# Decayed attention and a gated FFN on one core: loads, masks, weights and fillings moved at once

## The chip, the cores and the metric

The kernel runs on one core of a Trainium2 chip. The metric is the device time of one execution in microseconds (us); lower is better. The core has five engines that each run their own list of instructions strictly in order: TensorE (PE, with its weight loads as PEld), VectorE (DVE), ScalarE (ACT), GpSimd (POOL) and SyncE (SP). They meet only at semaphores. DMAs are issued from POOL (a software queue) or from SP (a hardware queue) and carried out by 16 DMA engines.

## The reference

Eight batches of eight heads, 576 positions, 64 wide; then a feed-forward block over all 4608 tokens of width 512. Cut to what matters:

```python
# attention: q, k, v (8, 8, 576, 64), f (8, 8, 576)
scores = q @ k.T / sqrt(64)
cum = cumsum(log(clip(f, 1e-4, 1)))
scores = where(causal, scores + cum[i] - cum[j], -1e9)
x = softmax(scores) @ v                    # tokens x (8*64 = 512)
# ffn: w_gate, w_val (512, 1536), w_out (1536, 512), rms_g (512)
xn = x / sqrt(mean(x*x) + 1e-6) * rms_g
g = xn @ w_gate
out = (g * sigmoid(g) * (xn @ w_val)) @ w_out      # (4608, 512) float32
```

## The kernel before

**Attention.** The decay exp(-cum[j]) does not depend on the query row, and exp(cum[i]) cancels in the softmax. So the kernel never adds the decay to the scores. At the start it works out `dec` = exp(-cum) for all 64 pairs of batch and head (f is loaded at L233; logarithm L257, scan L263, exp L268, transposed on PE at L277), and multiplies v by it (`scale_v`, L421; L422 writes the decay itself as a 65th column, which gives the denominator). A batch has five rows of 128 queries, j = 0 to 3 and a last one of 64. For each row and half of the heads come the scores on PE (L446), exp on ACT (L464), the mask of the diagonal block on POOL (L471, an affine select that writes zeros), the products with the scaled values on PE (L490), and a division by the 65th column on DVE (L504, L506), which gives a tile x of 128 tokens by 512.

q and k must stand transposed for the scores. For batches 0 and 1 PE does it (L392, L398, copied at L405); for the others SP issues DMA transposes (L377).

**Norm and FFN.** ACT squares x and adds up a row (L522); POOL divides by 512, adds 1e-6 (L526) and raises to the power -0.5 (L527); ACT scales x with it to xn (L534). xn is then transposed to xT: on PE with a copy by DVE for token groups 0 and 1 (L542, L550, L552), with DMA transposes from SP for the rest (L556). A token group g below 8 is the first 512 tokens of batch g; group 8 gathers the last 64 tokens of each batch (tile xTr). For every group PE multiplies xT with w_gate and w_val (L601), ACT takes a tanh (L613), DVE makes ga (L615) and hT (L608) of it, PE projects hT with w_out (L626), ACT copies the result out of the bank (L631), and SP stores it (L634). The products of both gates and of the projection, the transposes and the values share four accumulation banks ("ff"); the scores have two of their own.

**The RMS weights.** rms_g multiplies along the width of x. In group 0 the copy of xT does it (L550). After group 0 the function `weigh` (L340) multiplies both weight matrices in place, 24 operations of 128 x 512 on DVE, each third as soon as group 0 has used it; later groups then copy plainly.

**Loads and queues.** `load_qk` (L298) loads 128 rows of q or k, `load_qk2` (L310) 256 rows of them, `load_v` (L321) 128 rows of v, `load_w` (L331) a third of w_gate and of w_val, `load_wo` (L346) half of w_out. All are issued by POOL but the v of batch 1 and the first tile of batch 0, which SP issues. On each queue a DMA waits until the one eight before it has landed. Tiles for v are four in turn, those for scaled values two.

**The order.** The kernel builds a list of units, each with an engine, an assumed duration, a key and the tiles it takes and gives back. `Plan` plays them through on paper, at each step giving a free engine the unit with the lowest key that is ready, with a small random share in every key from a fixed seed. The units are then written out in that order, which each engine keeps. `fill` (L676) writes products of a constant tile ahead of units that by the plan leave PE idle in the first 25 us.

Of the kernel before, what the change touches and what calls it, by code (L numbers as in the profile page):

```python
# [10 lines left out]
F32 = mybir.dt.float32  # L11
# [6 lines left out]
class Unit:  # L18


    def __init__(self, eng, dur, key, emit, lat):
        self.eng, self.dur, self.key, self.emit, self.lat = eng, dur, key, emit, lat
        self.need, self.then, self.take, self.give = 0, [], [], []
# [9 lines left out]
class Plan:  # L33
# [20 lines left out]
    def fits(self, u):  # L54
        want = [h for h in u.take if h.slot is None]
        for h in want:
# [4 lines left out]
            elif n < sum(w.ring == h.ring for w in want):  # L61
                return False
# [12 lines left out]
    def run(self):  # L75
# [8 lines left out]
        draw = random.Random(149)  # L84
# [58 lines left out]
def fox_ffn_kernel(ctx, tc, q, k, v, f, moe_w_gate, moe_w_val, moe_w_out, moe_rms_g, out):  # L143
# [4 lines left out]
    NB = 5  # L148
# [10 lines left out]
    def ring(name, n, shape, dt, pool=sb):  # L159
# [3 lines left out]
                 sc=2, ff=4, hw=8, sw=8)  # L163
# [8 lines left out]
    T_x = ring("x", sizes["x"], [128, DM], F32)  # L172
# [18 lines left out]
    junk = sb.tile([128, DM], BF16, name="junk")  # L191
    warm = sb.tile([128, 128], BF16, name="warm")
    one = sb.tile([BH, 1], F32, name="one")
    mid = sb.tile([BH, 1], F32, name="mid")
    tmp = T_hT[1].rearrange("p f t -> p (f t)").bitcast(F32)
    fr, cum, dec = (tmp[0:BH, i * 640:i * 640 + n] for i, n in enumerate((S, S, NB * 128)))
    stat = [sb.tile([128, B, NB], F32, name=n) for n in ("sq", "ms", "rs")]
# [29 lines left out]
    PLAIN = 1  # L227

# [18 lines left out]
    def emit_ident():  # L247
        make_identity(nc, ident_f)
        nc.gpsimd.memset(mhalf, -0.5)

    dve(0.18, -30, lambda: nc.vector.memset(warm, 1.0))
    iden_f = pool(0.7, -15.5, emit_ident)
    iden = dve(0.23, -19, lambda: nc.vector.tensor_copy(ident, ident_f), [iden_f])

    d1 = dve(0.5, -19, lambda: nc.vector.tensor_scalar(fr, in0=fr, scalar1=1e-4, op0=ALU.max, scalar2=1.0,
                                                       op1=ALU.min), [L_f])
    d2 = act(0.7, -19, lambda: nc.scalar.activation(fr, fr, ACT.Ln), [d1])  # L257

    def emit_cum():
        ones = bass.AP(tensor=one.tensor, offset=one.offset, ap=[one.ap[0], [0, S]])  # L260
        nc.vector.memset(one, 1.0)
        nc.vector.memset(dec[:, S:], 0.0)
# [4 lines left out]
    d3 = dve(2.5, -19, emit_cum, [d2])  # L267
    d4 = act(0.9, -19, lambda: nc.scalar.activation(dec[:, 0:S], cum, ACT.Exp, scale=-1.0, bias=mid[:, 0:1]),  # L268
# [11 lines left out]
    d5 = pe(0.6, -19, emit_dect, [d4, iden_f], take=[h_dec])  # L280
    L_dec = dve(0.45, -19, lambda: nc.vector.tensor_copy(
# [32 lines left out]
    def load_v(b, j, key):  # L314
# [3 lines left out]
        eng, queue, dur = ("POOL", nc.gpsimd, 0.9) if b != 1 and b + j else ("SP", nc.sync, 0.6)  # L318
# [8 lines left out]
    def load_w(i, key):  # L327
        c0, c1 = i * 512, (i + 1) * 512
        for w, src, nm in ((wg, moe_w_gate, "g"), (wv, moe_w_val, "v")):
            def emit(w=w, src=src):  # L330
                nc.gpsimd.dma_start(out=w[:, :, c0:c1], in_=src[:, c0:c1].rearrange("(c p) f -> p c f", p=128))  # L331
            Lw[nm, i] = [load("POOL", 0.75, (512, 0.0061), key, emit, late=2.6)]

    def weigh(i, key, deps):

        c0, c1 = i * 512, (i + 1) * 512
        for w, nm in ((wg, "g"), (wv, "v")):
            def emit(w=w):
                for dc in range(NDC):
                    nc.vector.tensor_scalar_mul(w[:, dc, c0:c1], w[:, dc, c0:c1], rgT[:, dc:dc + 1])  # L340
            Lw[nm, i] = [dve(1.3, key, emit, deps[nm])]

    def load_wo(key):
        for i in range(2):
# [4 lines left out]
            Lo.append(load("POOL", 0.85, (768, 0.0061), key, emit))  # L349


    for at, (j, two) in ((-16, (0, False)), (-15, (1, True)), (-13, (3, False))):
        (load_qk2 if two else load_qk)(0, j, at)
        for i in range(j, j + 1 + two):
            load_v(0, i, at + 0.01)
    load_w(0, -14)
    load_w(1, -12)
    load_w(2, -11)
    load_wo(-9.25)
    for j in (0, 2):  # L360
        load_qk2(1, j, -9.5 + j * 0.1)
        load_v(1, j, -9.5 + j * 0.1)
        load_v(1, j + 1, -9.4 + j * 0.1)
# [70 lines left out]
    def score_block(tiles, key):  # L434
# [20 lines left out]
        for (b, qi, kjs, n), h in zip(tiles, holds):  # L455
# [12 lines left out]
            if kjs[-1] == qi:  # L468
# [4 lines left out]
                masked[b, qi].append(pool(0.15 + 0.95 * n / 128, key, mk, [e]))  # L473
# [3 lines left out]
    def values(b, qi, key):  # L477
        p0, n = rows(qi)
        hx = hold_x[b, qi] = Hold("x", 1)
        for par in range(2):  # L480
# [20 lines left out]
            def ev(par=par, hpo=hpo):  # L501
# [3 lines left out]
                d = T_x[hx.slot][0:n, :].rearrange("p (j a d) -> p j a d", a=2, d=D)[:, :, par, :]  # L505
# [214 lines left out]
```

## Time and profile before

| what | value |
|---|---|
| timed runs | 393.47, 397.14, 398.72 us; median 397.14 us |
| span of the profiled execution | 395.1 us, from the first to the last instruction |
| time of the profiled execution beside its span | not given apart; the median lies 2.0 us above the span |
| busy: PE, ACT, DVE, POOL | 370.0, 237.0, 219.6, 196.9 us |
| clock granted to PE, mean | 0.976 |
| moved by DMA | 44.84 MB, 113 GB/s over the span |

How to read it: the span runs from 0.0 at the first instruction. "L340" is line 340 of the kernel. In a row of a group stand line, engine, operation, out<-in by the program's names, shape, count, then busy us and mean ns of one, then idle time of the engine just before and what ended most of it. In a table by stage the granted clock is 1.00 at full speed.

### The profile page before, as it was taken

The page shows a single profiled execution, that of the slowest core. Times are in us where ns is not written, and L with a number is a line of the kernel's source. Part 1 is how long each engine was busy: PE and PEld are TensorE (multiplying, and loading weights), DVE is VectorE, ACT ScalarE, POOL GpSimd, SP SyncE. Part 2 cuts the span into 40 slices and gives each one's busy share as a digit, 9 for nine tenths or more (in the row PEclk, how much of TensorE's full clock was granted, in tenths as well). Part 3 has the DMA queues.
Part 4 walks back from the last instruction along what each step waited for, and adds up shares of the span by engine and source line. Part 5 has one row for each costly group of instructions (what it writes and reads, how often), then busy time and mean ns, then how long its engine had stood idle before and what let it go on. Part 6 is the DMA issues. An engine that isn't in the chain of part 4 may idle for free.

```text
span 395.1 us, 9891 instructions
## 1 busy us (share of the span) xinstructions
PE 370.0 (94%) x4044; PEld 221.4 (56%) x4044; DVE 219.6 (56%) x457; ACT 237.0 (60%) x377; POOL 196.9 (50%) x275
## 2 busy tenths in 40 slices
PE   5886989899996999999999999999999999999995
PEld 5775878678782544554555545554645454444442
DVE  4576988746451555664566457446653554555440
ACT  5474469687744866785678557865876532332221
POOL 8753539999963965695379466951221100000000
PEclk9599989999998999999999999999999999999998
DMA  9999999999998894999699999992021200001004
GB/s 133 191 200 190 198 142 113 151 182 175 167 124 93 112 181 79 146 150 179 69 131 149 141 116 106 180 175 62 9 54 56 55 33 29 27 27 55 28 26 106
DMA packets 133709, 44.84 MB, mean 113 GB/s; under 512 B 122432, under 2 KB 127040, under 8 KB 133664
## 3 DMA queue, kind: packets, MB, share of 16 engines
q0 software_dynamic: 76000, 22.16, 58.0%
q1 hardware_dynamic: 57136, 22.05, 32.3%
q8 instruction: 31, 0.51, 0.6%
q14 instruction: 14, 0.11, 0.1%
q10 hardware_dynamic: 528, 0.00, 0.1%
HBM read 37.90 MB, written 9.44 MB: 120 GB/s over the span
## 4 chain that ended last, share of the span: by engine, by line
PE 78%; DMA 6%; POOL 5%; DVE 5%; ACT 3%; issue 2%; SPq 0%; ACTq 0%; POOLq 0%
PE ff L601 42%; PE ff L626 23%; PE ff L490 6%; PE sc L446 6%; DMA v<-in_v_dram 3%; DMA xT<-xn 2%; POOL qk L298 2%; DVE wg L340 1%; ACT PT L464 1%; POOL v L321 1%; DVE wv L340 1%; ACT xn L534 1%; POOL PT L471 1%; PE sc L676 1%; POOL Vs L421 1%
## 5 line engine op out<-in xcount | busy, mean ns | idle before, releaser
L615 DVE SCALAR_TENSOR_TENSOR ga<-th,ff 128x512 f32<-128x512 f32 x108 | 73.8, 685 | 90.0 <-ACT th L613 88.5
L613 ACT ACTIVATE th<-ff 128x512 f32<-128x512 f32 x108 | 64.4, 596 | 77.8 <-PE ff L601 67.0
L626 PE MATMUL ff<-wo,hT 128*128 128x512 bf16 x432 | 109.9, 381 | 0.0
L464 ACT ACTIVATE PT<-sc 128x1024 bf16<-128x1024 f32 x96 | 95.3, 1021 | 23.0 <-PE sc L446 22.9
L601 PE MATMUL ff<-xT,wg 128*128 128x128 bf16 (+1 forms) x672 | 96.5, 288 | 7.6 <-DMA xT<-xn 4.2
L601 PE MATMUL ff<-xT,wv 128*128 128x128 bf16 (+1 forms) x672 | 98.9, 291 | 4.6 <-DVE x L506 3.8
L608 DVE SCALAR_TENSOR_TENSOR hT<-ga,ff 128x512 bf16<-128x512 f32 x108 | 73.2, 684 | 22.0 <-PE ff L601 20.3
L601 PEld LDWEIGHTS <-wg 128*128 128x128 bf16 x720 | 53.9, 98 | 45.3 <-DMA xT<-xn 4.7
L601 PEld LDWEIGHTS <-wv 128*128 128x128 bf16 x720 | 53.9, 99 | 41.5 <-issue 5.9
L471 POOL TENSOR_SCALAR_AFFINE_SELECT PT<-PT 128x1024 bf16<-128x1024 bf16 x32 | 35.3, 1103 | 67.3 <-ACT PT L464 67.2
L626 PEld LDWEIGHTS <-hT 128*128 128x128 bf16 x432 | 39.8, 98 | 43.5 <-issue 0.3
L490 PEld LDWEIGHTS <-PT 128*128 128x128 bf16 x896 | 38.4, 99 | 14.4 <-issue 1.3
L490 PE MATMUL ff<-Vs,PT 128*128 128x65 bf16 x896 | 42.6, 196 | 1.7 <-DVE x L506 0.8
L631 ACT COPY ores<-ff 128x512 f32<-128x512 f32 x36 | 21.0, 584 | 26.2 <-PE ff L626 26.2
L421 POOL TENSOR_TENSOR Vs<-v,decT 128x512 bf16<-128x512 f32 (+1 forms) x30 | 31.7, 1056 | 10.0 <-DMA v<-in_v_dram 8.9
L506 DVE TENSOR_TENSOR x<-ff,rden 128x256 f32<-128x256 f32 (+1 forms) x80 | 33.8, 423 | 2.8
L446 PE MATMUL sc<-QT,KT 64*128 64x128 bf16 (+1 forms) x960 | 34.4, 215 | 0.8 <-DVE QT L405 0.5
L446 PEld LDWEIGHTS <-KT 64*128 64x128 bf16 x960 | 25.1, 97 | 15.5 <-issue 11.7
L504 DVE RECIPROCAL rden<-ff 128x4 f32<-128x4 f32 (+1 forms) x80 | 14.3, 179 | 32.5 <-PE ff L490 31.8
L534 ACT ACTIVATE xn<-x,rs 128x512 bf16<-128x512 f32 (+1 forms) x40 | 27.5, 715 | 6.8 <-POOL rs L527 6.8
L522 ACT ACTIVATE junk<-x 128x512 bf16<-128x512 f32 (+1 forms) x40 | 25.1, 628 | 9.1 <-DVE x L506 9.0
L321 POOL DMA_DIRECT2D v<-in_v_dram x34 | 30.4, 895 | 0.0
(62 smaller groups left out, 239.5 us busy)
## 6 DMA issues: line engine op xcount, KB each, us to landing
out_dram<-ores SPq DMA_DIRECT2D x32, 256.0 KB, 2.6
v<-in_v_dram POOLq DMA_DIRECT2D x27, 256.0 KB, 6.0
qk<-in_k_dram POOLq DMA_DIRECT2D x26, 128.0 KB, 5.7
qk<-in_q_dram POOLq DMA_DIRECT2D x26, 128.0 KB, 5.8
wg<-in_moe_w_gate_dram POOLq DMA_DIRECT2D x3, 512.0 KB, 17.2
wv<-in_moe_w_val_dram POOLq DMA_DIRECT2D x3, 512.0 KB, 18.7
wo<-in_moe_w_out_dram POOLq DMA_DIRECT2D x2, 768.0 KB, 19.4
v<-in_v_dram SPq DMA_DIRECT2D x5, 256.0 KB, 10.2
```

The costliest lines, as they stand in the source:

```text
L321: queue.dma_start(out=T_v32[h.slot][0:n, :, :], in_=v[b, :, p0:p0 + n, :].rearrange("h p d -> p h d"))
L421: eng.tensor_tensor(T_Vs[hv.slot][0:n, j, :, 0:D], T_v32[h.slot][0:n, :, :], bcast(dj, D), ALU.mult)
L446: nc.tensor.matmul(t[:, par, c:c + n], lhsT=kt[r, p, kj * 128:(kj + 1) * 128], rhs=qt[r, p, qi * 128:qi * 128 + n], start=True, stop=True)
L464: nc.scalar.activation(T_of_p[hp.slot][:, 0:2 * half].rearrange("p (a c) -> p a c", a=2)[:, :, 0:cols], T_sc[h.slot][:, :, 0:cols], ACT.Ex ...
L471: nc.gpsimd.affine_select(out=d, in_=d, pattern=[[0, 8], [1, n]], compare_op=ALU.is_ge, fill=0.0, base=0, channel_multiplier=-1)
L490: nc.tensor.matmul(po[:, p, :], lhsT=T_of_p[h.slot][:, c:c + 128], rhs=vs[:, kj, 2 * p + par, :], start=(kj == 0), stop=(kj == qi))
L506: nc.vector.tensor_tensor(d, po[:, :, 0:D], bcast(r, D), ALU.mult)
L601: nc.tensor.matmul(T_ff[h.slot][:, c:c + n], lhsT=w[:, dc, fc * 128:(fc + 1) * 128], rhs=xT[:, dc, t0:t0 + n], start=(dc == 0), stop=(dc = ...
L608: nc.vector.scalar_tensor_tensor(hT, in0=three[0], scalar=0.5, in1=three[1], op0=ALU.mult, op1=ALU.mult)
L613: th = act(0.6, key - 0.1, lambda: nc.scalar.activation(T_th[ht.slot], T_ff[hg.slot], ACT.Tanh, scale=0.5), [ug], take=[ht])
L615: a = dve(0.72, key - 0.1, lambda: nc.vector.scalar_tensor_tensor(T_ga[ha.slot], in0=T_th[ht.slot], scalar=1.0, in1=T_ff[hg.slot], op0=ALU ...
L626: nc.tensor.matmul(T_ff[hf.slot], lhsT=T_hT[hold_hT[g].slot][:, fc, j * 128:(j + 1) * 128], rhs=wo[:, fc, :], start=(fc == 0), stop=(fc == ...
```

## The change

1. **v.** The v of batches 2 to 7 is issued by SP instead of POOL; the v of batch 1 by POOL instead of SP. The first tile of v stays with SP and now goes ahead of f.
2. **First loads.** The order was q, k of row 0; q, k of rows 1 and 2; v; the first third of the gate weights; q, k, v of row 3; the other thirds; w_out; batch 1. Now the first third of the gate weights comes right behind q and k of row 0, and batch 1 ahead of w_out.
3. **Masks and mean squares of batch 0.** The masks of its four full rows are a minimum with a constant tile `keep` (3e38 on and above the diagonal, 0 below) on DVE (L481). Its four full rows are squared and summed on DVE (L546). Every x tile has a 513th column that holds the square root of 512e-6, so that the sum contains the 1e-6, and the POOL operation for it (L526) goes in all batches.
4. **RMS weights.** `weigh` goes. rms_g is applied to x alone: in the copy of groups 0 and 1 (L572), and for the others by DVE behind the DMA transposes (L588), four operations of 128 x 256 for each pair of tiles, four of 128 x 64 for each piece of xTr.
5. **Fillings and order.** `fill` and its constant tile go. The table of exp is asked for right after the logarithm. A gate product starts in the plan only if one more bank is free (`spare`); at most two projections are under way; a part of a projection waits for its own third of hT only; the assumed cost of a weight load is 0.0053 instead of 0.0061, and the seed is 128 instead of 149.

```diff
-        draw = random.Random(149)
+        draw = random.Random(128)
...
+            nc.gpsimd.memset(t[:, DM:], (DM * 1e-6) ** 0.5)
...
-        eng, queue, dur = ("POOL", nc.gpsimd, 0.9) if b != 1 and b + j else ("SP", nc.sync, 0.6)
+        eng, queue, dur = ("POOL", nc.gpsimd, 0.9) if b < 2 and b + j else ("SP", nc.sync, 0.6)
...
-    def weigh(i, key, deps):
-        ...
-                for dc in range(NDC):
-                    nc.vector.tensor_scalar_mul(w[:, dc, c0:c1], w[:, dc, c0:c1], rgT[:, dc:dc + 1])
...
+                if b < 1 and n == 128:
+                    def mk(hp=hp):
+                        d = T_PT[hp.slot][:, 0:1024].rearrange("p (h q) -> p h q", q=128)
+                        m = bass.AP(tensor=keep.tensor, offset=keep.offset, ap=[keep.ap[0], [0, 8], [1, 128]])
+                        nc.vector.tensor_tensor(d, d, m, ALU.min)
+                    masked[b, qi].append(dve(0.65, key, mk, [e, keeps]))
...
-            nc.gpsimd.tensor_scalar(ms, in0=sq, scalar1=1.0 / DM, op0=ALU.mult, scalar2=1e-6, op1=ALU.add)
+        if b == 0 and js[0] < LAST:
+                nc.vector.scalar_tensor_tensor(junk, in0=t, scalar=1.0 / DM, in1=t, op0=ALU.mult, op1=ALU.mult,
+                                               accum_out=ms)
...
+                def wt(g=g, c0=c0, n2=n2):
+                    to = T_of[g][hold_xT[g].slot]
+                    for dc in range(NDC):
+                        nc.vector.tensor_scalar_mul(to[:, dc, c0:c0 + n2], to[:, dc, c0:c0 + n2], rgT[:, dc:dc + 1])
+                pieces[b, j] = dve(4 * (0.07 + n2 / 3840), key - 0.02, wt, pair + [L_rg])
...
+        ug.spare = 1
...
-            deps = hdone[g, j] + Lo if part == 0 else [last]
+            deps = hdone[g, j, part] + [Lo[part // 2]] + ([Lo[1]] if part == 1 else []) + ([last] if part else [])
...
-                if gap > 0.4 and u.at < 25:
-                    fill(u, 36 if gap > 4 else int(gap * 0.5 / 0.056))
```

What this does to the order is seen at three places. On POOL at the start, behind the first q and k, there stood before (wg and wv are the gate weights, PT the exponentials that are masked):

```order
L310 DMA qk_61<-in_q_dram 128x8x128
L310 DMA qk_62<-in_k_dram 128x8x128
L321 DMA v_84<-in_v_dram 128x8x64
L321 DMA v_85<-in_v_dram 128x8x64
L331 DMA wg<-in_moe_w_gate_dram 128x4x512
L331 DMA wv<-in_moe_w_val_dram 128x4x512
L298 DMA qk_67<-in_k_dram 128x8x64
L298 DMA qk_68<-in_q_dram 128x8x64
L321 DMA v_86<-in_v_dram 128x8x64
L331 DMA wg<-in_moe_w_gate_dram 128x4x512
L471 AFFINE_SELECT PT_89<-PT_89 128x1024
```

And there stands now, from the first weights on:

```order
L341 DMA wg<-in_moe_w_gate_dram 128x4x512
L341 DMA wv<-in_moe_w_val_dram 128x4x512
L253 MEMSET keep 128x128
L254 AFFINE_SELECT keep<-keep 128x128
L320 DMA qk_61<-in_q_dram 128x8x128
L320 DMA qk_62<-in_k_dram 128x8x128
L331 DMA v_84<-in_v_dram 128x8x64
L331 DMA v_85<-in_v_dram 128x8x64
L341 DMA wg<-in_moe_w_gate_dram 128x4x512
L341 DMA wv<-in_moe_w_val_dram 128x4x512
L308 DMA qk_67<-in_q_dram 128x8x64
L308 DMA qk_68<-in_k_dram 128x8x64
```

The weights' first third has moved ahead of q and k of rows 1 and 2, and no mask stands among the first loads.

On SP, around the transposes of batch 2 (KT, QT) and the first piece of group 8 (xTr), there stood before:

```order
L377 DMA_TRANSPOSE KT_82<-qk_65 128x4x128
L377 DMA_TRANSPOSE QT_79<-qk_66 128x4x128
L377 DMA_TRANSPOSE KT_82<-qk_67 128x4x128
L377 DMA_TRANSPOSE QT_79<-qk_68 128x4x128
L377 DMA_TRANSPOSE QT_79<-qk_69 128x4x64
L556 DMA_TRANSPOSE xTr_111<-xn_105 128x4x64
L377 DMA_TRANSPOSE KT_82<-qk_70 128x4x64
L634 DMA out_dram<-ores_118 128x512
```

And now:

```order
L381 DMA_TRANSPOSE KT_81<-qk_72 128x4x64
L331 DMA v_85<-in_v_dram 64x8x64
L381 DMA_TRANSPOSE QT_79<-qk_66 128x4x128
L381 DMA_TRANSPOSE KT_82<-qk_67 128x4x128
L576 DMA_TRANSPOSE xTr_111<-xn_105 128x4x64
L381 DMA_TRANSPOSE QT_79<-qk_68 128x4x128
L666 DMA out_dram<-ores_118 128x512
L381 DMA_TRANSPOSE QT_79<-qk_69 128x4x64
L331 DMA v_86<-in_v_dram 128x8x64
L331 DMA v_83<-in_v_dram 128x8x64
```

Loads of v, each of which waits for its tile, now stand between the transposes.

On DVE, where the attention of later batches runs beside the FFN of earlier groups, there stood before rows like these (ga and hT belong to the gates, rden and x to the attention):

```order
L615 SCALAR_TENSOR_TENSOR ga_116<-th_115,ff_124 128x512
L615 SCALAR_TENSOR_TENSOR ga_117<-th_114,ff_125 128x512
L608 SCALAR_TENSOR_TENSOR hT_112<-ga_116,ff_123 128x512
L608 SCALAR_TENSOR_TENSOR hT_112<-ga_117,ff_124 128x512
L615 SCALAR_TENSOR_TENSOR ga_116<-th_115,ff_126 128x512
L608 SCALAR_TENSOR_TENSOR hT_112<-ga_116,ff_123 128x512
```

And now, at the first piece of group 3:

```order
L647 SCALAR_TENSOR_TENSOR ga_116<-th_114,ff_126 128x512
L647 SCALAR_TENSOR_TENSOR ga_117<-th_115,ff_124 128x512
L639 SCALAR_TENSOR_TENSOR hT_112<-ga_116,ff_125 128x512
L588 TENSOR_SCALAR xT_110<-xT_110,rgT 128x256 x4
L639 SCALAR_TENSOR_TENSOR hT_112<-ga_117,ff_126 128x512
L515 RECIPROCAL rden_142<-ff_124 128x4
```

The weighing of x, which follows a DMA transpose, stands between operations that give back the banks of the gates.

More of the change, by code (lines that the diff above doesn't have):

```diff
@@ L22, in __init__ @@
         self.eng, self.dur, self.key, self.emit, self.lat = eng, dur, key, emit, lat
-        self.need, self.then, self.take, self.give = 0, [], [], []
+        self.need, self.then, self.take, self.give, self.spare = 0, [], [], [], 0
 class Hold:
@@ L60, in fits @@
                     return False
-            elif n < sum(w.ring == h.ring for w in want):
+            elif n < sum(w.ring == h.ring for w in want) + u.spare:
                 return False
@@ L225, in fox_ffn_kernel @@
     LEAD, SPAN = 0.3, 0.85
-    PLAIN = 1
     def akey(b, w):
```

142 lines of the change are left out of this document (75 added, 67 removed).

## The prediction

> **What bounds the kernel now.** I read the page's first lines, then busy time by stage, then the clock, then the chain of waits inside the stages where TensorE (PE) is not full.
>
> ```profile
> span 395.1 us, 9891 instructions
> PE 370.0 (94%) x4044; PEld 221.4 (56%) x4044; DVE 219.6 (56%) x457; ACT 237.0 (60%) x377; POOL 196.9 (50%) x275
> ```
>
> PE is busy 94% of the span. The table by stage (stretch, its length, then busy us with instruction counts for PE, PEld, DVE, ACT, POOL, then the granted clock, the DMA share and GB/s) shows where the rest is. I cut it at the first gate product (22.9), where the weights begin to be weighed, where they are done (74.0), and around the hole before token group 2.
>
> ```profile
> 0.00:22.90 22.90, 16.96 (x224) 14.69 (x225) 11.58 (x42) 13.37 (x17) 17.93 (x28) 0.78 1.28 168
> 22.90:44.80 21.90, 16.66 (x312) 15.19 (x313) 17.05 (x35) 11.41 (x20) 12.64 (x18) 1.00 1.38 193
> 44.80:74.00 29.20, 25.31 (x525) 22.50 (x520) 26.94 (x60) 20.91 (x30) 18.85 (x22) 0.94 1.30 148
> 74.00:118.10 44.10, 43.14 (x758) 34.81 (x756) 23.99 (x55) 32.67 (x54) 39.72 (x58) 1.00 1.63 158
> 118.10:128.00 9.90, 5.70 (x37) 2.58 (x37) 1.17 (x3) 4.30 (x8) 3.09 (x6) 0.83 0.93 99
> 128.00:390.30 262.30, 262.27 (x2202) 131.58 (x2200) 138.84 (x266) 153.75 (x251) 104.66 (x146) 1.00 0.68 91
> 390.30:395.10 4.80, 0.00 (x0) 0.00 (x0) 0.00 (x0) 0.59 (x1) 0.00 (x0) 0.79 0.47 109
> ```
>
> From 128.0 to 390.3 PE is full (262.27 of 262.30) at clock 1.00, so nothing taken off another engine can gain there, and what the change adds there costs only if it makes PE wait. All that can be won lies in the first 128 us, where DMA runs at 148 to 193 GB/s until 118. In the third stage VectorE (DVE) is nearly full: 26.94 of 29.20. The finer windows (PE busy, clock, DMA share, GB/s) show two cold spells after the start:
>
> ```profile
> 18.00:20.00 2.00, 2.00 (x30) 0.50 1.58 160
> ...
> 52.00:54.00 2.00, 1.20 (x20) 1.00 2.26 184
> 54.00:56.00 2.00, 0.94 (x10) 0.78 1.12 106
> 56.00:58.00 2.00, 2.00 (x32) 0.50 1.56 143
> ...
> 120.00:122.00 2.00, 0.00 (x0) 1.00 1.43 187
> ...
> 124.00:126.00 2.00, 2.00 (x20) 0.50 0.00 0
> ```
>
> A gap costs twice: its own time, then a few us at clock 0.50 behind it. The chain of waits (start, us, what) says what makes the gaps.
>
> ```profile
> 24.10 13.46 DMA v<-in_v_dram
> 37.59 0.70 DVE Vs L421
> ...
> 47.65 1.05 DVE wg L340 x4
> ...
> 50.49 1.54 DVE wv L340 x4
> ...
> 52.49 1.97 DVE wg L340 x4
> ...
> 112.94 9.34 DMA xT<-xn
> 122.33 1.04 PE ff L601 x4
> ```
>
> So: a v of batch 1 holds DVE near 37, weighing stands in the chain from 47, and a transpose that lands 9.34 us after its issue holds PE until 122.3.
>
> **The change part by part.** The sum is made against the profiled span of 395.1 us. The median of the timed runs, 397.14, is 2.0 above it, and I carry that 2.0 to the end.
>
> *First loads and fills.* The stage up to 44.8 has 44.80 − 16.96 − 16.66 = 11.2 us of idle PE, and part of its busy time is filling:
>
> ```profile
> L676 PE MATMUL ff<-warm 128*128 128x128 bf16 x74 | 7.2, 270 | 1.1 <-DVE warm L251 1.1
> L676 PE MATMUL sc<-warm 128*128 128x128 bf16 x29 | 3.0, 281 | 0.7 <-ACT PT L464 0.7
> L471 POOL TENSOR_SCALAR_AFFINE_SELECT PT<-PT 128x1024 bf16<-128x1024 bf16 x32 | 35.3, 1103 | 67.3 <-ACT PT L464 67.2
> L522 ACT ACTIVATE junk<-x 128x512 bf16<-128x512 f32 (+1 forms) x40 | 25.1, 628 | 9.1 <-DVE x L506 9.0
> L310 POOL DMA_DIRECT2D qk<-in_k_dram x1: 885/885/885, 26.5 to 26.5; - x1
> DMA to landing us min/median/max: 17.8/18.0/18.3
> ```
>
> The last q/k pair of batch 1 lands at 26.5 + 18.3 = 44.8. The loads that must be in by then are the same bytes less two v tiles of 256 KB, which now go behind: 512 KB at 193 GB/s is 2.7 us, so these could be in by 42. That is the end of gain, −3 us. Against it: part 0 of both gate weights, 2 × 512 KB, now goes ahead of the q and k of rows 1 and 2, which are then 1024 KB / 193 GB/s = 5.4 us later, and the attention rows of batch 0 with them. Batch 0's four masks leave POOL (1103 ns each) and its four squares leave ACT (628 each) for DVE, where the nearest row of an elementwise product, L550 below at 687 ns for 512 wide, bounds them at 0.69 to 1.4 a mask and takes 0.69 a square: 5.5 to 8.4 us, beside 11.58 busy of 22.90 and 17.05 of 21.90, so hidden but for the order. The 103 filling products, 10.2 us, go; they hide nothing but the cold clock. In the windows the clock was still 0.50 at 18 to 20 with PE full. Without fills the first full stretch starts with the first gates, so the clock comes up some us later: 4 us at 0.5 is 2 us of work lost. Bounds −3 and +7 (5.4 and 2); I take **+3**, nearer the delay because the rows of batch 0 are what the first gates wait for.
>
> *Weighing goes.* By groups:
>
> ```profile
> L340 DVE TENSOR_SCALAR wg<-wg,rgT 128x512 bf16<-128x512 bf16 x12 | 6.3, 590 | 0.0
> L340 DVE TENSOR_SCALAR wv<-wv,rgT 128x512 bf16<-128x512 bf16 x12 | 4.4, 428 | 0.0
> L340 DVE TENSOR_SCALAR wg<-wg,rgT x12: 341/346/1561, 47.6 to 69.7; 128x512 bf16<-128x512 bf16 x12
> L550 DVE TENSOR_TENSOR xT<-ff,rgT 128x512 bf16<-128x512 bf16 x4 | 2.7, 687 | 0.6 <-PE ff L542 0.6
> L552 DVE COPY xT<-ff 128x512 bf16<-128x512 bf16 x4 | 1.7, 424 | 3.7 <-PE ff L542 3.6
> ```
>
> 6.3 + 4.4 = 10.7 us of DVE between 47.6 and 72 go. Group 1's four copies become products: 4 × (0.687 − 0.424) = 1.1 us come. PE loses in 44.8 to 74: 29.20 − 25.31 = 3.9 us idle, and (1 − 0.94) × 29.20 = 1.75 to the clock, 5.6 in all. The three pieces of weighing that the chain shows ahead of the cold spell at 56 are 1.05 + 1.54 + 1.97 = 4.6 us. What is late next there is batch 1's chain of scores, exp and mask, which is not sped up. Bounds −1 (weighing lay beside that chain) and −6; I take **−4.5**, the chain's own pieces.
>
> *v on SP.* In POOL's groups of 60 to 118:
>
> ```profile
> L321 POOL DMA_DIRECT2D v<-in_v_dram x11 | 10.0, 913 | 0.0
> L526 POOL TENSOR_SCALAR ms<-sq 128x2 f32<-128x2 f32 (+1 forms) x6 | 1.4, 230 | 0.9 <-ACT junk L522 0.5
> ```
>
> POOL, busy 39.72 of 44.10 in 74 to 118, loses 11.4 us of issuing and mean squares. PE is idle there only 44.10 − 43.14 = 1.0 us: **−0.5**. The Trainium skill, "DMA: Bandwidth & Descriptors", section "Issuing engines are not separate DMA queues", says that moving an issue to another engine saves the issuing time alone, the transfers running on the same 16 DMA engines; by that rule the term is no more than these 11.4 us of POOL, and the trace has the room for it but nothing on whether the transfers get faster. Of new waits there is one: SP (L331 of the new kernel) now issues the v of batch 2's last row only when POOL has released its buffer, and behind it on SP stand batch 2's transposes and the first output; a hold there is a rival below.
>
> *The hole before group 2.* 118.1 to 128.0 loses 9.90 − 5.70 = 4.2 us idle and (1 − 0.83) × 9.90 = 1.7 of clock, 5.9 in all. The transposes of x:
>
> ```profile
> L556 SPq DMA_TRANSPOSE xT<-xn x24: 1189/1208/1650, 102.8 to 311.4; - x24
> DMA to landing us min/median/max: 2.4/4.5/9.3
> ```
>
> The one that made the hole landed in 9.34, the median is 4.5: 4.8 less would close 4.2 of idle and with it the cold spell. POOL, freed of 11.4 us, brings batch 2's scaled values and masks earlier, and projection parts that now wait only for their own third of hT are more cover for PE. The weighing of x by DVE stands in the path behind the transposes: four operations of 256 wide, between 0.17 (half of 346) and 0.35 each, I take 0.22: 0.9 us. −5.9 + 0.9 = **−5**; bounds −5.9 and 0.
>
> *x weights afterwards.* 12 pairs × 4 × 0.22 = 10.6 us, and 32 narrow operations for the last tokens (64 wide, between an eighth of 346 ns and all of it: 1.4 to 11 us), on a DVE that has 262.3 − 138.8 = 123.5 us free: **0**, with +4 as the other end where a pair lands just before its product. The Trainium skill, "SBUF — State Buffer", section "SBUF: two separate sides", says that a VectorE operation in a two-port mode and a GpSimd one lock each other out for a whole instruction. The trace agrees as far as weighing goes: the same 128×512 operation took 341 to 1561 ns. By it the weights would run up to 4.5 times longer while POOL works, 10.6 → 48 us, still under the free 123.5.
>
> The rule on spare banks, the ring of two projections and the other seed only reorder: nothing after 128, where PE has no gap to fill, and ahead of it they lie within the bounds above. The tail, 4.8, stays. Sum: 3 − 4.5 − 0.5 − 5 + 0 = −7.0, 388.1 of span, and with 2.0 **390.1 us**.
>
> **The rivals.**
>
> *A. Slower: DVE stands still behind x weights.* DVE runs strictly in order, and a weight waits for a DMA, which no DVE instruction of the steady part did. Queued behind it are the ga and hT operations that give back PE's four product banks:
>
> ```profile
> L615 DVE SCALAR_TENSOR_TENSOR ga<-th,ff 128x512 f32<-128x512 f32 x108 | 73.8, 685 | 90.0 <-ACT th L613 88.5
> 80.05 0.89 PE ff L601 x16
> ```
>
> PE can run on for about two products, 2 × 0.89 = 1.8 us, then it waits. A weight that comes to its turn right as its transpose is issued holds DVE for the 4.5 us median: 4.5 − 1.8 = 2.7 us lost. Of the 20 weights (12 pairs, 8 small) seven so placed make 7 × 2.7 = 19 us: 390 + 19 = 409. It decides from a hold over 1.8 us. For: transposes land late whenever loads run, up to 9.3. Against: loads thin out (DMA share 1.63 in 74 to 118, 0.68 from 128 on), and in the order the weights stand among attention rows that come after the transposes were issued. Chance 0.17.
>
> *B. The hole stays, or SP is late.* If v on SP waits for POOL, the x transposes behind land as late as before: the term −5 becomes 0, 395; with the start at +7 too, 399. For: SP gets 26 issues more, and each x transpose keeps it 1.2 us. Against: POOL is freed. Chance 0.17.
>
> *C. No warm clock at the start.* PE kept clock 1.00 in the stage from 22.9 to 44.8 at 16.66 / 21.90 = 76% load, but it had come there with fills. If the sparser work without them holds it at 0.50 for 12 us of that stage, half of them is lost, 6 more: 396.1. Chance 0.05. The Trainium skill, "TensorE: Matmul & The Clock Gate", section "Part 1: The HAM clock gate", has half speed as the default, released after about 3.4 us of activity and lost after an idle window; it speaks against removing fills, and the trace agrees with its second half: after the empty 120 to 122 the clock was 0.50.
>
> *D. The start gains too.* DVE no longer stands behind batch 1's late v (13.46 us to landing in the chain), and v arrives in the order of use: −3 instead of +3, 384.1, and with the third stage at −6, 382.6. Chance 0.18.
>
> **How the numbers follow.** The forecast, 384 to 395, has 0.43, and its middle is 390. A measurement of this kernel tells 2% from no change: below 389.2 is faster, above 405.1 slower. Faster: D, 0.18, and the half of the forecast that lies below 389.2, 0.22: 0.40. Slower: A but for the few holds that stay under 405.1, 0.15, and 0.01 of B: 0.16. Within: the rest, 0.44. The range goes from 380 (D with the hole wholly shut is 381.7, and the three timed runs lie 3.7 and 1.6 around their median, so 2 more) to 404 (B at its end is 399.1; A with five holds is 390 + 13.5); outside lie about 0.05 below and 0.15 above.
>
> **What would show it.** The weighing line gone, and no stretch at clock 0.50 around 55, would show the second term; if PE still loses over 4 us between 45 and 74, it is wrong. The first gate before 22 and the first gate of row 3 after 46 show the first term both ways. The hole: the longest idle of PE between 100 and 130 under 1.5 us, and what ends it. For A: DVE idle time ended by the x transposes, with PE waiting for hT or ga behind it, and PE under 99% after 130. If PE is full after 130 and the time is still above 397, the start lost it, and the forecast's signs are wrong there.

## The result and the profile after

The changed kernel takes 391.85 us (median of 20 runs, 387.03 to 397.09), the kernel before 395.18 (20 runs, 391.32 to 398.72). The ratio is 0.9927 with a 95% interval of 0.9898 to 0.9956: 0.7% faster, clear of noise and well under 2%. The ratio compares undisturbed runs alone, which is why the medians of all runs stand 0.8% apart. The forecast was 390.1 in a range of 380 to 404. The profiled execution has a span of 388.2 (forecast 388.1) against 395.1. These two executions lie further apart than the kernels: the one after took 389.89 us, 2.0 under its median, and the one before, if it too had 1.7 us beside its span, some 396.8, which is 1.6 over its median. So the stages below share out 6.9 us where the medians differ by 3.3.

First the table by stage of the changed kernel, with the columns and cuts of the prediction's table (the last two cuts follow its own end):

```profile
0.00:22.90 22.90, 9.41 (x104) 7.21 (x105) 12.52 (x40) 9.94 (x12) 16.54 (x33) 1.00 1.24 170
22.90:44.80 21.90, 18.30 (x389) 16.32 (x388) 19.22 (x45) 15.84 (x21) 13.96 (x18) 1.00 1.42 216
44.80:74.00 29.20, 25.41 (x467) 20.02 (x466) 17.94 (x39) 21.59 (x35) 18.89 (x25) 1.00 1.87 154
74.00:118.10 44.10, 42.44 (x784) 36.37 (x783) 29.20 (x68) 31.67 (x50) 27.81 (x36) 1.00 1.35 146
118.10:128.00 9.90, 9.90 (x91) 5.10 (x89) 5.35 (x16) 8.56 (x17) 7.23 (x10) 1.00 1.36 135
128.00:384.00 256.00, 253.82 (x2117) 127.53 (x2114) 149.24 (x317) 147.39 (x241) 80.78 (x107) 1.00 0.70 92
384.00:388.20 4.20, 0.00 (x0) 0.00 (x0) 0.00 (x0) 0.00 (x0) 0.00 (x0) 0.61 0.32 74
```

The hole at 118 to 128 is gone: TensorE (PE) is busy 9.90 of 9.90 at clock 1.00, where it had 5.70 at 0.83. VectorE (DVE) fell from 26.94 to 17.94 in the third stage and rose from 11.58 and 17.05 to 12.52 and 19.22 in the first two. POOL, 39.72 of 44.10 in the fourth, has 27.81.

PE's busy time counts filling products and slow ones alike. So that stages can be compared, I counted PE's own work in both traces: each product of 128 columns at 56 ns and of 512 at 216 ns, the pace at full clock, the narrower ones likewise, without fillings. Both traces hold all of it, 342.2 us. Work done by a time:

| by (us) | before | after | lead of after | forecast of the stage | came out as |
|---|---|---|---|---|---|
| 22.9 | 4.2 | 4.2 | 0.0 | | |
| 44.8 | 19.2 | 20.1 | 0.9 | loses 3 | gains 0.9 |
| 74.0 | 40.1 | 43.5 | 3.4 | gains 4.5 | gains 2.5 |
| 118.1 | 81.3 | 84.5 | 3.2 | gains 0.5 | loses 0.2 |
| 128.0 | 85.3 | 94.0 | 8.7 | gains 5 | gains 5.5 |
| the end | 342.2 | 342.2 | 6.9 (span) | 0 | loses 1.8 |

Between these two executions four fifths of the gain, 5.5 of 6.9 us, lie in ten microseconds around the first product of token group 2.

What PE, DVE and POOL wait for in the changed kernel (engine, line, what ends the wait: us in all, times, longest):

```profile
POOL Vs L425 <- DMA v<-in_v_dram: 21.9, 13, 4.3
...
DVE xT L588 <- DMA xT<-xn: 3.5, 5, 1.5
...
DVE xTr L588 <- DMA xTr<-xn: 3.3, 2, 2.8
...
PE ff L632 <- issue: 1.9, 1, 1.9
PE ff L632 <- DVE ga L647: 1.8, 2, 1.7
```

The 4.2 us that PE waited for a transpose of x are no longer there. In their place stand new waits on other engines: POOL for v, now issued by SP (8.9 us before), and DVE for the transposes whose result it weighs. The chain of waits around 78 shows the second of them at work (start, us, what):

```profile
74.31 4.28 DMA xTr<-xn
78.58 0.02 issue
78.61 1.52 DVE xTr L588 x4
80.13 0.60 DVE ga L647
80.73 0.04 issue
80.77 1.05 PE ff L632 x16
```

DVE stands behind a piece of xTr that lands after 4.28 us; the ga queued behind it gives a bank back late, and PE has no bank for 1.7 us. That is rival A of the prediction, once and small.

### The profile page after: what moved, and what is told of

Read it like the earlier page. It is cut to its first block, busy times and chain, and to the rows that moved or that the text cites. A ratio compares the mean times of both kernels' runs of the same rounds, so it can differ in the third digit from the quotient of the medians.

```text
span 388.2 us, 9775 instructions
## 1 busy us (share of the span) xinstructions
PE 359.3 (93%) x3941; PEld 212.5 (55%) x3941; DVE 233.5 (60%) x524; ACT 235.0 (61%) x370; POOL 165.2 (43%) x228
## 3 DMA queue, kind: packets, MB, share of 16 engines
q1 hardware_dynamic: 80576, 27.95, 40.1%
## 4 chain that ended last, share of the span: by engine, by line
PE 77%; DMA 15%; POOL 3%; issue 1%; DVE 1%; ACT 1%; SPq 1%; ACTq 0%; POOLq 0%; DVEq 0%
PE ff L632 42%; PE ff L658 23%; PE ff L501 7%; PE sc L450 5%; DMA qk<-in_k_dram 4%; DMA wv<-in_moe_w_val_dram 3%; DMA v<-in_v_dram 3%; DMA xT<-xn 2%; DMA QT<-qk 2%; DMA xTr<-xn 1%; POOL qk L308 1%; POOL v L331 0%; POOL qk L320 0%; DVE xT L588 0%; DVE xTr L588 0%
## 5 line engine op out<-in xcount | busy, mean ns | idle before, releaser
L658 PE MATMUL ff<-wo,hT 128*128 128x512 bf16 x432 | 108.3, 379 | 0.6 <-DVE xT L572 0.6
L632 PE MATMUL ff<-xT,wv 128*128 128x128 bf16 (+1 forms) x672 | 97.2, 289 | 1.8 <-DVE ga L647 1.8
L632 PEld LDWEIGHTS <-wg 128*128 128x128 bf16 x720 | 54.9, 99 | 43.3 <-issue 4.3
L475 POOL TENSOR_SCALAR_AFFINE_SELECT PT<-PT 128x1024 bf16<-128x1024 bf16 x28 | 30.7, 1096 | 69.0 <-ACT PT L468 47.4
L501 PEld LDWEIGHTS <-PT 128*128 128x128 bf16 x896 | 37.0, 98 | 15.8 <-DVE PT L481 2.0
L425 POOL TENSOR_TENSOR Vs<-v,decT 128x512 bf16<-128x512 f32 (+1 forms) x30 | 31.4, 1046 | 26.6 <-DMA v<-in_v_dram 21.9
L450 PE MATMUL sc<-QT,KT 64*128 64x128 bf16 (+1 forms) x960 | 33.4, 211 | 2.3 <-ACT KT L409 1.2
L450 PEld LDWEIGHTS <-KT 64*128 64x128 bf16 x960 | 24.1, 95 | 15.9 <-issue 12.0
L308 POOL DMA_DIRECT2D qk<-in_q_dram x34 | 29.7, 874 | 2.1 <-POOLq L722 0.8
L308 POOL DMA_DIRECT2D qk<-in_k_dram x34 | 29.1, 857 | 2.1 <-DMA wv<-in_moe_w_val_dram 1.2
## 6 DMA issues: line engine op xcount, KB each, us to landing
qk<-in_q_dram POOLq DMA_DIRECT2D x26, 128.0 KB, 5.9
qk<-in_k_dram POOLq DMA_DIRECT2D x26, 128.0 KB, 6.3
```

Of the source, the lines that this page charges most:

```text
L308: nc.gpsimd.dma_start(out=T_qk[h.slot][0:n, :].rearrange("p (h d) -> p h d", d=D), in_=src[b, :, p0:p0 + n, :].rearrange("h p d -> p h d"))
L425: eng.tensor_tensor(T_Vs[hv.slot][0:n, j, :, 0:D], T_v32[h.slot][0:n, :, :], bcast(dj, D), ALU.mult)
L450: nc.tensor.matmul(t[:, par, c:c + n], lhsT=kt[r, p, kj * 128:(kj + 1) * 128], rhs=qt[r, p, qi * 128:qi * 128 + n], start=True, stop=True)
L475: nc.gpsimd.affine_select(out=d, in_=d, pattern=[[0, 8], [1, n]], compare_op=ALU.is_ge, fill=0.0, base=0, channel_multiplier=-1)
L501: nc.tensor.matmul(po[:, p, :], lhsT=T_of_p[h.slot][:, c:c + 128], rhs=vs[:, kj, 2 * p + par, :], start=(kj == 0), stop=(kj == qi))
L632: nc.tensor.matmul(T_ff[h.slot][:, c:c + n], lhsT=w[:, dc, fc * 128:(fc + 1) * 128], rhs=xT[:, dc, t0:t0 + n], start=(dc == 0), stop=(dc = ...
```

## The experiments

Each kernel below keeps the order of the kernel it comes from, and only what a planned step writes is altered, but for the last three, which are planned anew. Ratios are to the kernel before, with 95% intervals.

### The changed kernel again

> The changed kernel once more, as the yardstick for the runs beside it. Both theories: 0.990 to 0.996 of the kernel before; span about 388.

391.26 us; ratio 0.9925 (0.9888 to 0.9961), span 388.8. It is the yardstick. Its waits differ in place from those above: the first piece of xTr, issued at 74.3 in both, lands after 2.3 us here, DVE does not stand, and PE has no gap at 80; instead it waits 1.16 us at 124. Two executions of one kernel thus lose a microsecond or two in different places.

### The hole: eight loads of batch 3 left out

```diff
# kernel before
             def emit(src=src, h=h):
+                if b == 3 and h.slot in full:   # a tile that an earlier batch filled
+                    return
                 nc.gpsimd.dma_start(out=T_qk[h.slot][0:n, :]...
```

> The kernel before in its own order, with 8 of the 10 loads of q and k of batch 3 left out (their tiles keep what an earlier batch loaded, so the results of batch 3 are not computed). In the kernel before, these loads start at 109 to 113, amid the last two transposes of x for group 2, and the last of these lands after 9.3 us; in the changed kernel they start behind it and it lands after 3.7. If the collision makes the hole, the last transpose lands in 3 to 5 us, TensorE's wait of 4.2 near 118 falls under 1, and the time falls by 3 to 5 us (ratio 0.987 to 0.993). If the hole comes from the lack of work in front of it alone (rival), 0 to 1.5 us: 0.996 to 1.000.

391.14 us against 395.99; ratio 0.9932 (0.9898 to 0.9965): as much as the whole change. PE's wait for a transpose of x and the stage of the hole in this kernel:

```profile
PE ff L607 <- DMA xT<-xn: 0.6, 1, 0.6
```

```profile
118.00:128.00 10.00, 9.95 (x108) 5.11 (x108) 6.25 (x14) 8.63 (x16) 8.85 (x11) 1.00 1.08 114
```

The hole is gone with its cold spell. But this run does not test the collision, because the expectation names the wrong loads. In the order of issue 14 loads of q and k stand ahead of batch 2's, and then come ten for each batch. So the four at 109 to 113 are batch 4's, and the eight left out are batch 3's, which the kernel before issues at 74 to 98. Batch 4's four still run amid the last pair of transposes of x. First the kernel before, with the landing times of the transposes, then this kernel:

```profile
L298 POOL DMA_DIRECT2D qk<-in_q_dram x2: 903/938/972, 109.4 to 113.0; - x2
L298 POOL DMA_DIRECT2D qk<-in_k_dram x2: 885/890/896, 110.3 to 112.1; - x2
L556 SPq DMA_TRANSPOSE xT<-xn x2: 1212/1226/1241, 111.0 to 112.9; - x2
...
DMA to landing us min/median/max: 6.8/8.1/9.3
```

```profile
L304 POOL DMA_DIRECT2D qk<-in_q_dram x2: 913/935/957, 107.8 to 111.4; - x2
L304 POOL DMA_DIRECT2D qk<-in_k_dram x2: 887/895/903, 108.8 to 110.5; - x2
...
L562 SPq DMA_TRANSPOSE xT<-xn x2: 1199/1202/1206, 109.0 to 110.9; - x2
...
DMA to landing us min/median/max: 4.9/5.7/6.5
```

The last transpose is issued 2.0 us earlier and lands after 6.5 us instead of 9.3, so 4.9 us earlier in all. PE's work in front of group 2's first product hardly grows: 5.4 us for 4.9 after that issue. What the left-out loads gave was room further ahead, as the DMA share (the last figure but one) shows, before and then here:

```profile
98.00:104.00 6.00, 5.55 (x119) 4.74 (x117) 1.70 (x5) 4.97 (x10) 5.80 (x10) 1.00 1.74 154
```

```profile
98.00:104.00 6.00, 6.00 (x133) 5.46 (x132) 3.18 (x7) 5.24 (x9) 5.97 (x10) 1.00 0.58 97
```

They also spare POOL eight issues and the DMA engines 0.9 MB. So in this run the hole closes as the transposes land earlier, and that came about with batch 4's loads still beside them. Which of the things spared did it, this run can't part.

In the changed kernel batch 4's loads start behind the last pair. In its yardstick run, the tile's transposes from SP in the window around that pair:

```profile
L576 SPq DMA_TRANSPOSE xT<-xn x2: 1189/1197/1205, 109.9 to 111.2; - x2
...
DMA to landing us min/median/max: 3.7/4.1/4.6
```

Worked out from the traces: the kernel before issues the last transpose at 112.9 with batch 4's q and k issued from 109.4 to 113.0, and has 4.9 us of PE work until group 2's first product; the changed kernel issues it at 111.2 with q and k from 112.6 on, and has 7.8 us of work. Both the landing (9.3 to 3.7) and the cover (4.9 to 7.8) moved, by the order. The other traces go the same way. Where three or four of these loads were issued in the 4.4 us ahead of the last transpose, it landed after 6.5 to 9.6 us (five traces, of the kernel before and its variants); where none to two were, after 3.0 to 5.9 us (nine traces, of the changed kernel and its variants). That these loads hold the transpose up is therefore likely, but no run moved them alone.

### v from SP, apart

```diff
# kernel before
-            queue.dma_start(out=T_v32[h.slot][0:n, :, :], ...
+            (nc.sync if b > 1 else queue).dma_start(out=T_v32[h.slot][0:n, :, :], ...
```

> The kernel before in its own order, with the v of batches 2 to 7 issued from SP. If freeing POOL brings batch 2 forward, as the forecast has it, the hole near 118 shrinks by over 2 us and the time by 2 to 4: 0.990 to 0.995. If v on SP is worth nothing by itself, or stands in the way of the transposes behind it, the hole stays at 3 to 5 us: 0.998 to 1.006.

396.31 us; ratio 1.0044 (1.0008 to 1.0080): a little slower. In its trace, of an execution of 399.60 us, PE's wait at group 2's first product is 4.0 us, about as before. So freeing POOL of the issues of v, 10.0 of the 11.4 us that the forecast counts, is not what closes the hole, and that reason of the forecast falls. Its other reason, more work as cover, is not touched by this run.

```diff
# changed kernel
-            queue.dma_start(out=T_v32[h.slot][0:n, :, :], ...
+            (nc.gpsimd if b > 1 else queue).dma_start(out=T_v32[h.slot][0:n, :, :], ...
```

> The changed kernel in its own order, with the v of batches 2 to 7 issued from POOL again. If late v from SP (POOL waited 21.9 us for v where it had waited 8.9) is what holds TensorE near 124 through POOL, ScalarE and VectorE, this gains 1 to 2 us on the changed kernel (ratio to the kernel before 0.987 to 0.990). If the issue time saved on POOL is worth more, as the forecast's third term has it (-0.5), it loses 0.5 to 3 us: 0.994 to 1.000.

391.96 us; ratio 0.9996 (0.9929 to 1.0062). The interval lies above the 0.987 to 0.990 that the first theory expects, so moving v back gives nothing back; it holds all of the second's 0.994 to 1.000, and whether SP's issue is worth anything stays open. In its trace POOL waits no less for v with the issue moved back, and PE more for weighed x.

```profile
POOL Vs L425 <- DMA v<-in_v_dram: 25.4, 12, 4.5
...
PE ff L632 <- DVE xT L588: 2.9, 2, 2.1
```

### Weighing, apart

```diff
# kernel before
             def emit(w=w):
-                for dc in range(NDC):
-                    nc.vector.tensor_scalar_mul(w[:, dc, c0:c1], w[:, dc, c0:c1], rgT[:, dc:dc + 1])
+                pass
```

> The kernel before in its own order, with the weighing of the gate weights (24 operations, 10.7 us of VectorE between 47 and 72) left out; the computation then leaves rms_g out for token groups 1 to 8. If the forecast's second term is right, this alone gains 3.5 to 5 us on the kernel before (ratio 0.987 to 0.991) and the cold clock near 56 is gone. If weighing lay beside other work (rival), 0 to 1.5 us: 0.996 to 1.000. The changed kernel's lead over the kernel before between 44.8 and 74, by work done on TensorE, grew by 2.1 us only, so I expect the middle: 0.993 to 0.996.

392.74 us against 396.51; ratio 0.9977 (0.9928 to 1.0026): anything from 0.7% gained to 0.3% lost, and not the 3.5 to 5 us of the forecast's term. The two stages that matter, in a trace of this kernel whose execution took 396.15 us, 3.4 above its median:

```profile
44.80:74.00 29.20, 27.31 (x581) 23.76 (x580) 18.97 (x42) 24.14 (x36) 21.90 (x26) 1.00 1.42 153
118.10:128.00 9.90, 7.67 (x43) 3.28 (x44) 1.93 (x5) 3.13 (x4) 2.08 (x4) 0.66 0.29 29
```

In its own stage the term holds: PE 27.31 for 25.31 at clock 1.00 for 0.94, and the cold spell near 56 is gone. But the hole behind it grew: PE's wait for the transpose of x is 5.5 us for 4.2 and the clock 0.66 for 0.83. In this execution what was won ahead of the hole was waited away in it: the last transpose was issued at 110.7, 2.2 us earlier than in the kernel before, but took 9.6 us and landed only 2.0 us earlier, while PE was out of work 3.3 us earlier. That other executions lose it in the same place is not shown.

```diff
# changed kernel
                 def wt(g=g, c0=c0, n2=n2):
-                    to = T_of[g][hold_xT[g].slot]
-                    for dc in range(NDC):
-                        nc.vector.tensor_scalar_mul(to[:, dc, c0:c0 + n2], ...
+                    pass
```

> The changed kernel in its own order, without the weighing of x by VectorE behind the transposes; the computation then leaves rms_g out for token groups 2 to 8. The forecast has this weighing at 0 to 1 us in all (0.9 in front of group 2): ratio to the changed kernel 0.997 to 1.001. The rival that VectorE stands still in order behind late transposes has the two holds that TensorE shows (1.7 us near 80, 0.9 near 151) and their like: 3 to 6 us less, ratio 0.985 to 0.993.

390.06 us; ratio 0.9897 (0.9844 to 0.9951), beside 0.9925 (0.9888 to 0.9961) for the changed kernel in the same job. The weighing of x costs 1.2 us by the medians; the intervals overlap, so it may cost nothing, or some 3 us. The 19 us of rival A are excluded. Without DVE's holds PE waits elsewhere: 2.8 us at 124 for a ga. The stretch of the trace that shows why (start, us, engine, line, operation, then idle time before it and what ended it):

```profile
120.47 1.04 POOL L425 TENSOR_TENSOR Vs<-v,decT 128x512 bf16<-128x512 f32 x1 [5.71 <-DMA v<-in_v_dram]
...
121.61 0.57 POOL L551 TENSOR_TENSOR rs<-ms,mhalf 64x1 f32<-64x1 f32 x1
...
122.22 0.72 ACT L557 ACTIVATE xn<-x,rs 64x512 bf16<-64x512 f32 x1 [3.87 <-POOL rs L551]
122.85 0.57 ACT L643 ACTIVATE th<-ff 128x512 f32<-128x512 f32 x1
...
123.45 0.69 DVE L645 SCALAR_TENSOR_TENSOR ga<-th,ff 128x512 f32<-128x512 f32 x1 [6.40 <-ACT th L643]
124.19 0.60 PE L501 MATMUL ff<-Vs,PT 128*128 128x65 bf16 x8 [2.81 <-DVE ga L645]
```

A late v stops four engines in turn, each because its next instruction stands in order behind one that waits: POOL in Vs, with rs behind; ACT in xn, with the tanh behind; DVE in ga; PE for the bank.

### Masks and mean squares of batch 0, apart

```diff
# changed kernel
-                    masked by nc.vector.tensor_tensor(d, d, m, ALU.min)
+                    masked by nc.gpsimd.affine_select(...)          # rows 0 to 3 of batch 0
-                nc.vector.scalar_tensor_tensor(junk, in0=t, ..., accum_out=ms)
+                nc.scalar.activation(junk, t, ACT.Square, scale=DM ** -0.5, accum_out=ms)
```

> The changed kernel in its own order, with batch 0's four masks back on POOL and its four mean squares back on ScalarE. If these were worth something at the start, the first gate of group 0 comes 0.4 us later for the first mask and the time grows 1 to 3 us (ratio 1.003 to 1.008). If they are hidden, as the forecast has it, 0.998 to 1.002.

391.48 us; ratio 0.9935 (0.9897 to 0.9973), as the changed kernel. Yet they are not hidden where they stand; the stage from 22.9 to 44.8, first with them back on POOL and ACT, then in the changed kernel again:

```profile
22.90:44.80 21.90, 17.22 (x340) 15.43 (x333) 16.43 (x35) 16.41 (x24) 15.10 (x20) 0.92 1.41 218
```

```profile
22.90:44.80 21.90, 18.28 (x392) 16.21 (x390) 19.21 (x45) 16.15 (x21) 13.93 (x18) 1.00 1.41 217
```

392 products at clock 1.00 for 340 at 0.92. By 74 the counted work is the same in both, 41.9 us, so the gain is waited away before that; in the changed kernel's run PE waits 1.3 us for a transposed q near 60. (These later traces lack some 47 matmul records each, so their counts are compared with one another only.)

### Fillings, apart

```diff
# changed kernel
+                gap, pe_end = u.at - pe_end, u.at + u.dur
+                if gap > 0.4 and u.at < 25:
+                    fill(u, 36 if gap > 4 else int(gap * 0.5 / 0.056))
```

> The changed kernel in its own order, with the filling products put back in front of the units that by the plan leave TensorE idle in the first 25 us. If the missing fills cost about 2 us at the start (a late clock, the forecast's first term), this gains 1 to 3 us on the changed kernel (ratio to it 0.992 to 0.997) and the first gate product takes 0.9 us instead of 1.9. If fills only fill (rival), the ratio is 0.998 to 1.005.

```diff
# kernel before
-                if gap > 0.4 and u.at < 25:
+                if False:
```

> The kernel before in its own order, without the 103 filling products. With fills put into the changed kernel the time rose by 0.9% instead of falling. If fills delay TensorE's own work at the start, this gains 1 to 3 us on the kernel before (0.992 to 0.997). If they warm the clock and the rise had another cause, such as one execution's late transposes near 80 and 126, it loses 0 to 2 us (1.000 to 1.005).

With fillings the changed kernel takes 394.86 us, ratio 0.9991 (0.9951 to 1.0031); without them the kernel before takes 395.34, ratio 1.0060 (1.0020 to 1.0100). The signs disagree: put in, they cost some 0.7%; taken out, they cost 0.6%. What they do at once is plain; the first gate product and the one behind it, with fillings and then without:

```profile
20.25 1.07 PE L634 MATMUL ff<-xT,wg 128*128 128x128 bf16 x16
21.15 1.06 PE L634 MATMUL ff<-xT,wv 128*128 128x128 bf16 x16
```

```profile
20.62 1.89 PE L632 MATMUL ff<-xT,wg 128*128 128x128 bf16 x16
22.31 1.22 PE L632 MATMUL ff<-xT,wv 128*128 128x128 bf16 x16
```

They warm the clock, and PE is 1.1 us of work ahead at 22.9 (5.4 for 4.3). By 44.8 both have 20.3. In between PE waits in both for exp and masks, for xn, and for DVE; what stands behind those waits was not followed. The rest of the difference lies past 76, in waits like the one at 80 (2.0 us with fillings; without, none in that job and 1.7 in the first profile). Whether fillings shift these by a fixed mechanism or the traces show single executions stays open.

### The order, planned anew

```diff
-        draw = random.Random(128)
+        draw = random.Random(149)
```

> The changed kernel with the old seed for the random share of the keys, so that only the order differs. If the order by chance is worth little, 0.990 to 0.996 of the kernel before, as the changed kernel. If the seed is what the gain hangs on, 0.997 to 1.010.

392.03 us; ratio 0.9968 (0.9923 to 1.0013). It can be told neither from the changed kernel (0.9925) nor from the kernel before, so how much of the gain hangs on the seed stays open.

```diff
-    load_w(0, -29)
+    load_w(0, -27.5)
```

> The changed kernel with one key altered: the first third of the gate weights is loaded behind q, k and v of rows 1 and 2, as in the kernel before; the order is planned anew with it. By the forecast's first term (rows 1 and 2 come 5.4 us late behind these weights, +3 of loss), this gains 1 to 4 us by 45 us. By what the trace after shows (1.6 us more of TensorE's work done by 44 than before), the new order is the better one, and this loses 0 to 3 us at 44; in the end time 0.993 to 1.002 of the kernel before.

400.83 us; ratio 1.0150 (1.0092 to 1.0207), far outside both expectations. By 44.8 the forecast was right: with q, k and v of rows 1 and 2 ahead of the first weights PE has done 21.8 us of work for 20.3, and by 74 it has 45.0 for 41.9. Then everything is lost at once: by 118.1 it has 76.6 for 83.1. The longest of PE's waits there is rival A again:

```profile
101.65 0.68 DVE L588 TENSOR_SCALAR xTr<-xTr,rgT 128x64 bf16<-128x64 bf16 x4 [2.72 <-DMA xTr<-xn]
...
102.91 1.57 PE L632 MATMUL ff<-xT,wv 128*128 128x128 bf16 x16 [2.51 <-DVE x L517]
```

DVE stands 2.7 us for a piece of xTr, and behind it stands the division that gives x and a bank back. PE waits 2.5 us and goes on at a slower pace, 1.57 us for 16 products.

```diff
-                pieces[b, j] = dve(..., wt, pair + [L_rg])       # for each piece of xTr
+            deps = [dve(1.4, 7.5, wt8, [pieces[b, LAST] for b in range(B)] + [L_rg])]
```

> The changed kernel with the last tokens' tile weighed once, 4 operations of 128 x 512 ahead of group 8, instead of 32 of 128 x 64 behind each of its eight transposes; the order is planned anew. VectorE then cannot stand behind the first of these transposes near 78, where it held TensorE for 1.7 us in one profile. If such holds are what is left to gain, 0.5 to 2 us less than the changed kernel: 0.988 to 0.992 of the kernel before. If they come and go without an effect on the end, 0.990 to 0.996.

400.55 us; ratio 1.0167 (1.0122 to 1.0212): 28 operations less and 9 us slower than the changed kernel. The stretch of the trace in which it happens, and the clock of the two windows of 4 us from 96 on (PE, PEld, DVE, ACT, POOL busy, clock, DMA share, GB/s):

```profile
96.91 1.04 POOL L425 TENSOR_TENSOR Vs<-v,decT 128x512 bf16<-128x512 f32 x1 [4.24 <-DMA v<-in_v_dram]
...
98.05 0.69 POOL L551 TENSOR_TENSOR rs<-ms,mhalf 128x2 f32<-128x2 f32 x1
...
98.71 1.08 POOL L475 TENSOR_SCALAR_AFFINE_SELECT PT<-PT 128x1024 bf16<-128x1024 bf16 x1
...
99.85 0.69 PE L501 MATMUL ff<-Vs,PT 128*128 128x65 bf16 x13 [3.02 <-POOL PT L475]
```

```profile
96.00:100.00 4.00, 0.98 (x41) 0.81 (x41) 0.00 (x0) 1.23 (x2) 2.88 (x4) 1.00 0.70 120
100.00:104.00 4.00, 3.47 (x52) 3.20 (x50) 1.21 (x4) 3.63 (x7) 0.66 (x1) 0.52 0.37 80
```

Again a v from SP is late, now in front of a mask that PE needs: 3 us idle, and the clock falls to 0.52. The hole that the changed kernel closed at 118 opens at 96 in another order.

## Why the prediction was right, and where its steps were not

The sign came out, and the time lies near the forecast, 391.85 for 390.1. The size did not come out as well. The forecast took 7.0 us off 397.14, the median of three runs; over 20 runs the kernel before has 395.18, and the change takes 3.3 us off it by the medians, 0.7% by the ratio. So the forecast gain is over twice the measured one, and a starting point 2.0 us too high made up for part of it. The spans agree, 388.2 for 388.1, only because the two profiled executions lie further apart than the kernels. In the sum the errors of the terms, −3.9, +2.0, +0.7, −0.5 and +1.8, cancel to +0.1: that it came out so close is luck.

- **First loads, fills, masks: +3 forecast, −0.9 measured.** The step that failed is "hidden but for the order": batch 0's masks and squares on DVE let PE run 392 products for 340 in the second stage, so they were a gain there, not a cost at nothing, though in the end time the gain does not show (0.9925 with them on DVE, 0.9935 without). The delay of rows 1 and 2 behind the weights is real, 1.5 us by 44.8 for 5.4 of transfer (20.3 for 21.8), mis-sized rather than wrong. Of the late clock, 2 us forecast, 1.1 showed at 22.9 and none at 44.8.
- **Weighing: −4.5 forecast, −2.5 measured in its stage.** The chain's 4.6 us of weighing were not all PE's: without weighing, the kernel before gains 2.0 us of PE time there and its cold spell goes, and in that trace it gives this back in the hole. The forecast summed stages as if a gain passed through; a later wait on a transfer can absorb it.
- **v on SP: −0.5 forecast, +0.2 measured**, and 1.0044 (1.0008 to 1.0080) alone. The term was small and of the wrong sign. The Trainium skill, "DMA: Bandwidth & Descriptors", section "Issuing engines are not separate DMA queues", says that another engine's issue saves issuing time alone. The traces agree: v from SP took 5.8 us to land in the median, from POOL 6.0 before.
- **The hole: −5 forecast, −5.5 measured.** The landing fell from 9.3 to 3.7, more than forecast (median 4.5 taken). Of the two reasons given, POOL's freed time is not enough: without the issues of v on POOL the hole stays. More work as cover came true, 7.8 us for 4.9. What the forecast did not see is that batch 4's loads moved behind the transposes. Whether that, the earlier issue or the cover was decisive stays open: leaving out loads of batch 3 closes the hole as well (0.9932, 0.9898 to 0.9965), with batch 4's loads in place.
- **x weights afterwards: 0 forecast with +4 as the end, +1.8 measured** for all losses past 128. They took 281 ns for 256 wide, not 220, and 235 for 64 wide.
- **Rivals.** A came at two places, 1.7 us at 80 and 0.9 in all near 154, not at seven. Its sum of a hold less 1.8 us was too small: a hold of 2.8 made 1.7, and the weighing behind the hold took another 1.52. In the order with q, k and v first it cost 2.5 us more. B's price was not paid, but its wait, late v on SP, appeared in POOL at 21.9 us. C lasted for one product and a half. D was half right: the start gained 0.9, not 3.

## What to carry to other kernels

A stage's gain counts only if no later wait on something unmoved, such as a transfer, absorbs it: price each stage up to the next such wait, and look there first. Where a transfer lands late, ask which loads were issued in the few microseconds before it, and count them off by batch before blaming one: an experiment that leaves out the wrong loads can still give the time hoped for. With engines that keep their order, one late tile stops every engine that has queued behind it, so a planned order must be measured anew after each edit: two edits that took work or delay away cost over 2% against the changed kernel.

## What the runs showed of the hardware

- The granted clock in the rows is not always the pace. In the changed kernel it reads 1.00 from 0 to 128, but the first 16 products of a gate at 20.6 took 1.89 us and later ones 1.05 to 1.07. So a row of 1.00 at the start does not tell the pace, and the products' own times must be read.
- PE can stand in the middle of a product with nothing to wait for. In five kernels it stops 1.6 to 2.2 us between the 6th and the 7th of 16 products near 66 (first start and us of both parts, from the second run of the changed kernel):

```profile
65.80 0.50 PE L632 MATMUL ff<-xT,wg 128*128 128x128 bf16 x6
...
67.96 0.73 PE L632 MATMUL ff<-xT,wg 128*128 128x128 bf16 x10 [1.66 <-issue]
```

  One instruction transfer begins between 65 and 66, while the DMA engines are full with batch 2's transposes and with loads. With the fillings in, the stop is at another instruction, 1.1 us earlier. That PE waits for its own code fits, but was not tested.
- DVE's weighing of 64 columns took 235 ns at the median, of 256 columns 281 and of 512 (in the kernel before) 346: most of it does not depend on the width, and splitting such work costs almost by the piece.
